# Sparse linear layer: the first weight piece in four row transfers on two queues, and the sixth token tile's load moved to ScalarE's queue

## The chip, the cores and the metric

One core of a Trainium2 chip. The metric is the device time of one execution in microseconds (us), lower is better; the median of several runs is compared. All starts below are us from the start of the profiled span. "Landed" is when a transfer's semaphore was complete, "issued" when the issuing engine began the DMA instruction.

## The reference

```
B, S, D = x.shape                      # x (16, 512, 1024), w (1024, 1024), b (1024), bf16
wg = w.reshape(D // 4, 4, D)           # groups of 4 neighbouring input rows
mag = jnp.abs(wg)
thr = second largest of mag in each group, for each output column
wp = (wg * (mag >= thr)).reshape(D, D) # keep 2 of 4
return jnp.einsum("bsd,df->bsf", x, wp) + b
```

So the weights have to be pruned on the chip before they can be used, and then 8192 tokens are multiplied by a 1024 x 1024 matrix.

## The kernel before, in words

The tokens are 64 tiles of 128. The output columns are two halves `h` of 512, the input rows two halves `g` of 512. A group's four rows lie side by side in the free dimension of the weight tiles `w_gh[(g, h)]` (128 partitions x 4 rows `m` x 512 columns), so that pruning is elementwise work on VectorE.

The front works on weight pieces: `pieces` 0 and 1 are columns 0 to 256 and 256 to 512 of `g` = 0, pieces 2 and 3 the next two quarters, pieces 4 and 5 the two halves of `g` = 1. For a piece, `abs_piece` takes the magnitude (an AND with 0x7FFF on VectorE, for piece 0 in two instructions, rows 0 and 1 and then rows 2 and 3; piece 3 on ScalarE), `prep_piece` computes the threshold (L131 to L138), the mask (L145) and the pruned weights (L148), for piece 0 again by two rows at a time. `load_w` (L71) loads columns of weights; it takes a range of rows `m0:m1`.

While pieces are pruned, TensorE transposes the first eight token tiles itself: `load_x` (L79) loads the first 512 columns of one or two token tiles, `transpose_half` (`T.t` in the list, four matmuls at L175) transposes tile `t` into a PSUM bank, `copy_half` (`C.t`, L180) copies it out on ScalarE, and `mm_part` (`N` and `M`, L196) multiplies it with a pruned piece. The tiles are counted from 0, so the sixth tile is tile 5.

The order of everything in the front is written out by hand in the string `FRONT`: each engine does its part of the list in that order. It begins with ten warm-up matmuls of 512 columns and two of 128 (`W`, `w`, L105), which need no data, and then

```
T.0 T.1 C.0 T.2 T.3 C.1 w T.4 T.5 C.2 N.0.0.0 N.0.0.1
N.0.1.0 N.0.1.1 N.0.2.0 N.0.2.1 N.0.0.2 N.0.0.3 ...
```

`N.0.t.m` is the product of tile `t` with row `m` of piece 0. The list then goes on with `C.4 C.5 M.0.3 N.0.4.0.1 T.6 T.7`, pieces 1 to 5, six further tiles whose tokens come by a transposing DMA (`xfill`, `load_fill`, L252), and copies of the pruned weights into their natural order `wp_nat` by DMA (`unpack`, `U`, L165). Partial sums are staged in SBUF (`to_stage`, `add_stage`, `add_bias`).

From 56 us on (L364) the remaining tiles run in batches of eight with transposing DMAs `xTb` two batches ahead (`issue_batch`, L264), 16 matmuls of 512 columns for each tile, and VectorE adding the bias out of PSUM (L241). Results of two tiles share a buffer `o_pair` (five of them); `half_done` writes a pair with one DMA of 512 KB from ScalarE's queue (L221), or, for the pairs in `singly`, with one of 256 KB after each tile (L214, L217).

Loads are issued by SyncE (SP) unless another engine is given; SyncE issues nearly all of them, in program order. Before the change ScalarE issues rows 2 and 3 of piece 0 and the tokens of tiles 2 and 3, then loads its function table, does a copy of 16 columns (`act_first`, L100), and turns to `C.0`. `K` keeps each engine's instructions in program order.

Of the kernel before, what the change touches and what calls it, by code (L numbers as in the profile page):

```python
# [10 lines left out]
def kernel(  # L11
# [7 lines left out]
    nc = tc.nc  # L19
# [49 lines left out]
    def load_w(g, c0, c1, eng=nc.sync, m0=0, m1=4):  # L69
        dst = w_gh[(g, c0 // FH)][:, m0:m1, c0 % FH:c0 % FH + c1 - c0]  # L70
        K(eng.dma_start(dst, wv[:, g, m0:m1, c0:c1]))  # L71
# [4 lines left out]
    def load_x(ta, tb, eng=nc.sync):  # L76
        xt = const.tile([P, tb - ta, KH], bf16, name=f"xh_{ta}")
        src = xf[ta * P:tb * P, 0:KH].rearrange("(t p) c -> p t c", p=P)
        K(eng.dma_start(xt[:], src))  # L79
        for t in range(ta, tb):  # L80
            xh[t] = xt[:, t - ta, :]

    load_w(0, 0, 256, nc.sync, 0, 2)
    load_w(0, 0, 256, nc.scalar, 2, 4)
    load_x(0, 2)
    load_x(2, 4, nc.scalar)
    load_x(4, 5)
    load_x(5, 6)
    load_w(0, 256, 512)
    load_x(6, 8)  # L90
    load_w(0, 512, 1024)
    bias_sb = const.tile([P, Dout], bf16, name="bias_sb")

    xg1 = const.tile([P, 4, T * P], bf16, name="xg1")
# [3 lines left out]
    K(nc.vector.memset(zeros[:], 0.0))  # L98
    act_first = const.tile([P, 16], bf16, name="act_first")
    K(nc.scalar.copy(act_first[:], zeros[:]))  # L100
    ident = const.tile([P, P], bf16, name="ident")
    make_identity(nc, ident[:])

# [100 lines left out]
            o_left[t // 2] = 2 if t == NT - 2 else 4  # L204
        return o_pair[t // 2][:, t % 2, :]

    singly = range(10, 17)

    def half_done(t):
        p = t // 2  # L210
# [188 lines left out]
```

## Time and profile before

| | |
|---|---|
| time, median of 3 runs | 233.31 us (233.16 to 233.41) |
| the profiled execution: its time / its span | 233.16 us / 231.4 us |
| TensorE busy | 227.9 us (98%) |
| VectorE, ScalarE, GpSimd busy | 120.4, 18.0, 0.7 us |
| DMA | 38.19 MB, mean 165 GB/s |
| granted TensorE clock | 0.999 |
| first matmul / first transpose (`T.0`) / first product (`N.0.0.0`) | 0.77 / 4.78 / 6.57 us |

The transfers of the first microseconds:

| transfer | queue | issued | landed |
|---|---|---|---|
| piece 0, rows 0 and 1 (128 KB) | SyncE | 0.73 | 3.53 |
| piece 0, rows 2 and 3 (128 KB) | ScalarE | 0.74 | 3.76 |
| tokens of tiles 0, 1 (256 KB) | SyncE | 1.25 | 4.74 |
| tokens of tiles 2, 3 (256 KB) | ScalarE | 1.26 | 5.24 |
| tokens of tile 4 (128 KB) | SyncE | 1.75 | 5.69 |
| tokens of tile 5 (128 KB) | SyncE | 2.25 | 6.07 |
| piece 1 (256 KB) | SyncE | 2.73 | 6.91 |
| tokens of tiles 6, 7 (256 KB) | SyncE | 3.44 | 8.67 |
| pieces 2 and 3 (512 KB) | SyncE | 4.10 | 11.02 |
| piece 4 (512 KB) | SyncE | 4.71 | 12.38 |
| `xfill`, first half (transposing) | SyncE | 5.38 | 16.77 |

In the profile PE is TensorE, PEld its weight loads, DVE VectorE, ACT ScalarE, POOL GpSimd, SP SyncE; a "q" behind the name means that the engine's issue side is meant. `q1` is SyncE's DMA queue and `q10` ScalarE's. A line of the timeline gives start, length, engine, source line, operation, output and input, and a count where like instructions are put together. Matmuls overlap: one of 256 columns is listed with 0.27 us, but the next begins 0.109 us later.

### The profile page before, as it was taken

Reading aid. Unit: us, or ns where it says so; the run is one execution under the profiler, and the core shown is the slowest. Engines: PE = TensorE matmul, PEld = TensorE weight load, DVE = VectorE, ACT = ScalarE, POOL = GpSimd, SP = SyncE. Lnnn points to the kernel's source line nnn. Section 1 sums busy time; section 2 is a strip of 40 time slices with the busy share of each in tenths; the row PEclk is TensorE's granted clock in tenths of the full one; section 3 lists DMA queues with packets and bytes.
Section 4 is the critical chain, followed back from the end, with each engine's and each line's share of the span. In section 5 each row is a group of like instructions: output and inputs, shape, how many; then the busy total and the mean of one; then the engine's idle time right before and its main releaser. Section 6 shows DMA issues by size and latency. Waiting matters only on the chain.

```text
span 231.4 us, 2786 instructions
## 1 busy us (share of the span) xinstructions
PE 227.9 (98%) x1156; PEld 110.8 (48%) x1156; DVE 120.4 (52%) x208; ACT 18.0 (8%) x33; POOL 0.7 (0%) x6
## 2 busy tenths in 40 slices
PE   8999999999999999999999999999999999999995
PEld 4887444444444444444444444444444444444443
DVE  3899887867987424424424424423423433433434
ACT  3777500000000000000000000000000000000000
POOL 1000000000000000000000000000000000000000
PEclk9999999999999999999999999999999999999999
DMA  6989998999957222991259622696129961122222
GB/s 208 264 179 233 218 192 177 267 258 270 320 189 272 91 95 70 235 284 58 81 129 251 164 93 92 137 241 192 68 91 200 224 211 40 53 91 91 91 93 91
DMA packets 77100, 38.19 MB, mean 165 GB/s; under 512 B 63136, under 2 KB 68896, under 8 KB 77088
## 3 DMA queue, kind: packets, MB, share of 16 engines
q1 hardware_dynamic: 67712, 20.91, 44.5%
q10 hardware_dynamic: 9376, 17.11, 20.4%
q8 instruction: 9, 0.15, 0.3%
q14 instruction: 3, 0.02, 0.0%
HBM read 3.41 MB, written 16.78 MB: 87 GB/s over the span
## 4 chain that ended last, share of the span: by engine, by line
PE 98%; DVE 0%; issue 0%
PE bank L364 73%; PE bank L196 17%; PE bank L256 6%; PE bank L105 2%; PE bank L175 1%; DVE o_last L347 0%
## 5 line engine op out<-in xcount | busy, mean ns | idle before, releaser
L364 PE MATMUL bank<-wp_nat,xTb 128*128 128x512 bf16 x752 | 162.5, 379 | 0.0
L241 DVE TENSOR_TENSOR o_pair<-bank,bias_sb 128x512 bf16<-128x512 f32 x104 | 67.3, 686 | 99.5 <-PE bank L364 96.3
L364 PEld LDWEIGHTS <-xTb 128*128 128x128 bf16 x752 | 73.6, 98 | 88.7
L232 DVE TENSOR_TENSOR stage<-bank,stage 128x512 f32<-128x512 f32 x22 | 14.4, 687 | 3.4 <-PE bank L196 3.3
L196 PE MATMUL bank<-w,xT 128*128 128x256 bf16 x128 | 14.5, 273 | 0.0
L196 PE MATMUL bank<-wp_nat,xg 128*128 128x512 bf16 x64 | 14.1, 379 | 0.0
L236 DVE TENSOR_TENSOR o_pair<-stage,bias_sb 128x512 bf16<-128x512 f32 x22 | 14.0, 683 | 0.0
L196 PEld LDWEIGHTS <-xT 128*128 128x128 bf16 x128 | 12.2, 98 | 1.8 <-ACT xT L180 0.2
L228 ACT COPY stage<-bank 128x512 f32<-128x512 f32 x22 | 11.4, 611 | 3.7 <-PE bank L196 3.7
L196 PE MATMUL bank<-wp_nat,xfill 128*128 128x512 bf16 x48 | 10.7, 379 | 0.0
L256 PE MATMUL bank<-wp_nat,xfill 128*128 128x512 bf16 x48 | 10.5, 379 | 0.0
L196 PEld LDWEIGHTS <-xg 128*128 128x128 bf16 x64 | 6.3, 98 | 7.5
L256 PEld LDWEIGHTS <-xfill 128*128 128x128 bf16 x48 | 4.7, 97 | 5.7
L196 PEld LDWEIGHTS <-xfill 128*128 128x128 bf16 x48 | 4.7, 98 | 5.4
L364 PE MATMUL bank<-wp_nat,xTs 128*128 128x512 bf16 x32 | 7.1, 379 | 0.0
L145 DVE TENSOR_TENSOR mask<-mag,thr 128x512 bf16<-128x512 bf16 (+2 forms) x9 | 5.5, 630 | 0.2
L148 DVE TENSOR_TENSOR w<-w,mask 128x512 bf16<-128x512 bf16 (+2 forms) x9 | 5.5, 630 | 0.2
L105 PE MATMUL bank<-const-bfloat16-1.0 128*128 128x512 bf16 (+1 forms) x12 | 4.4, 542 | 0.8 <-PEq L383 0.8
L364 PEld LDWEIGHTS <-xTs 128*128 128x128 bf16 x32 | 3.1, 98 | 3.8
L120 DVE TENSOR_SCALAR mag<-w 128x512 uint16<-128x512 uint16 (+2 forms) x6 | 2.7, 468 | 3.1 <-DMA w<-in_w_dram 3.1
L180 ACT COPY xT<-bank 128x512 bf16<-128x512 bf16 x8 | 4.1, 607 | 2.8 <-PE bank L175 2.8
L256 PE MATMUL bank<-wp_nat,xTb 128*128 128x64 bf16 (+3 forms) x40 | 3.7, 251 | 0.0
(20 smaller groups left out, 26.4 us busy)
## 6 DMA issues: line engine op xcount, KB each, us to landing
out_dram<-o_pair ACTq DMA_DIRECT2D x24, 512.0 KB, 2.8
out_dram<-o_pair ACTq DMA_DIRECT2D x15, 256.0 KB, 2.1
wp_nat<-w SPq DMA_DIRECT2D x16, 128.0 KB, 2.9
w<-in_w_dram SPq DMA_DIRECT2D x3, 512.0 KB, 6.9
xh<-in_x_dram SPq DMA_DIRECT2D x2, 256.0 KB, 4.4
xh<-in_x_dram ACTq DMA_DIRECT2D x1, 256.0 KB, 4.0
xh<-in_x_dram SPq DMA_DIRECT2D x2, 128.0 KB, 3.9
w<-in_w_dram SPq DMA_DIRECT2D x1, 256.0 KB, 4.2
```

The source lines that it names most:

```text
L105: K(nc.tensor.matmul(bank[7][:, :n], lhsT=ones[:, :P], rhs=ones[:, :n], start=True, stop=True))
L120: K(nc.vector.tensor_single_scalar(mag[:, ms].bitcast(u16), w_of(i)[:, ms].bitcast(u16), 0x7FFF, op=Alu.bitwise_and))
L145: K(nc.vector.tensor_tensor(mask[:, ms], mag[:, ms], tb, op=Alu.is_ge))
L148: K(nc.vector.tensor_tensor(w_of(i)[:, ms], w_of(i)[:, ms], mask[:, ms], op=Alu.mult))
L180: K(nc.scalar.copy(xt[:], src))
L196: K(nc.tensor.matmul(dst, lhsT=lhs, rhs=rhs, start=c0 == 0 and m == 0, stop=c1 == FH and m == 3))
L228: K(nc.scalar.copy(stage[(h, t)][:], bank[own[(h, t)]][:]))
L232: K(nc.vector.tensor_tensor(st, bank[own[(2 + h, t)]][:], st, op=Alu.add))
L236: K(nc.vector.tensor_tensor(get_o(t)[:, f], stage.pop((h, t))[:], bias_sb[:, f], op=Alu.add))
L241: K(nc.vector.tensor_tensor(get_o(t)[:, f], bank[bk][:], bias_sb[:, f], op=Alu.add))
L256: K(nc.tensor.matmul(bank[bk][:, :c1 - c0], lhsT=xN[t][:, kt, :], rhs=wp_nat[h][:, kt, c0:c1], start=kt == 0, stop=kt == KT - 1))
L364: K(nc.tensor.matmul(bank[bks[h]][:], lhsT=xN[t][:, kt, :], rhs=wp_nat[h][:, kt, :], start=kt == 0, stop=kt == KT - 1))
```

## The change

Piece 0 is loaded by four transfers of one row each, rows 0 and 2 from SyncE and rows 1 and 3 from ScalarE. The tokens of tile 5 are issued by ScalarE, after its first copy in program order, and no longer by SyncE between tile 4 and piece 1. In program order the loads of tiles 6 and 7 and of pieces 2 and 3 now stand behind that; on SyncE's own queue their order is the same. Pairs 10 and 11 of the output are written as pairs.

```diff
-    load_w(0, 0, 256, nc.sync, 0, 2)
-    load_w(0, 0, 256, nc.scalar, 2, 4)
+    for m in range(4):
+        load_w(0, 0, 256, nc.scalar if m % 2 else nc.sync, m, m + 1)
     load_x(0, 2)
     load_x(2, 4, nc.scalar)
     load_x(4, 5)
-    load_x(5, 6)
     load_w(0, 256, 512)
-    load_x(6, 8)
-    load_w(0, 512, 1024)
     bias_sb = const.tile([P, Dout], bf16, name="bias_sb")
...
     K(nc.scalar.copy(act_first[:], zeros[:]))
+    load_x(5, 6, nc.scalar)
+    load_x(6, 8)
+    load_w(0, 512, 1024)
     ident = const.tile([P, P], bf16, name="ident")
...
-    singly = range(10, 17)
+    singly = range(12, 17)
```

## The prediction

> **What bounds the kernel now.** I read the page's busy shares first, then the chain of waits, then the timeline of the first 10 us by engine, and last the transfers one by one. T0, T1, ... are the token tiles; "T5's transposes" are the four L175 matmuls of the sixth tile.
>
> ```profile
> PE 227.9 (98%) x1156; PEld 110.8 (48%) x1156; DVE 120.4 (52%) x208; ACT 18.0 (8%) x33; POOL 0.7 (0%) x6
> PE 98%; DVE 0%; issue 0%
> ...
> PEld L196 <- ACT xT L180: 0.2, 1, 0.2
> PEld L175 <- DMA xh<-in_x_dram: 0.2, 1, 0.2
> ```
>
> TensorE starts at 0.77 and never stops; only two short waits after the warm-up stand on its side. So the time is TensorE's stream plus the holes in it, and the whole effect of the change must be a hole opened or closed. Holes to close: the starts of the single matmuls, where they are further apart than their own 109 ns or 56 ns, give 0.05 us at 6.57 (first product, pruned rows ready at 6.52), 0.06 at 7.07 (C.2's copy), 0.01 at 7.19, 0.07 at 7.37 (second half of the pruned rows), 0.07 at 8.71 to 8.80 (T6's load), 0.03 at 10.3 to 10.4: 0.29 us, of which 0.24 lie behind the first product. That is all that any earlier load can win.
>
> ```profile
> 4.78 1.40 PE L175 MATMUL bank<-ident,xh 128*128 128x128 bf16 x16
> 6.02 0.22 PE L105 MATMUL bank<-const-bfloat16-1.0 128*128 128x128 bf16 x1
> 6.07 0.61 PE L175 MATMUL bank<-ident,xh 128*128 128x128 bf16 x8
> 6.57 2.27 PE L196 MATMUL bank<-w,xT 128*128 128x256 bf16 x18
> 8.71 0.64 PE L175 MATMUL bank<-ident,xh 128*128 128x128 bf16 x8
> ```
>
> Read this against the landings: T0 begins at 4.78 with its load landed at 4.74; T5 begins at 6.30 with its load landed at 6.07 (cover 0.23); T6 begins at 8.71 with its load at 8.67. TensorE's order is fixed: T5's transposes stand in front of all products, so if T5's tokens are late, everything is late.
>
> ```profile
> xh<-in_x_dram SPq DMA_DIRECT2D x1, 128.0 KB, 3.8
> ...
> w<-in_w_dram SPq DMA_DIRECT2D x1, 256.0 KB, 4.2
> ...
> 1.79 1.28 ACT L100 ACT_TABLE_LOAD   x1 [1.79 <-issue]
> 3.09 0.20 ACT L100 COPY act_first<-zeros 128x16 bf16<-128x16 bf16 x1
> ...
> q10 hardware_dynamic: 85, 0.09, 96.7%
> q1 hardware_dynamic: 18, 0.01, 12.7%
> ```
>
> The first two are T5's load (issued 2.25, landed 6.07) and the second weight piece (issued 2.73, landed 6.91). The last two are the queues between 4.00 and 4.25: ScalarE's queue (q10), with T2/T3's load issued at 1.26, takes 85 packets, while SyncE's (q1) nearly stands still, though T4's load was issued on it at 1.75. Landings come in the order of issue over both queues: 3.53, 3.76, 4.74, 5.24, 5.69, 6.07, 6.91, 8.67. So I treat the two queues as one line, in which place goes by time of issue. The data run 3 to 4 us behind the issue: a transfer issued a little later loses nothing unless it loses its place.
>
> **The change, part by part.**
>
> *Four row transfers for two.* Same 256 KB. SyncE's list keeps its count up to the first weight pieces (two rows, T0/T1, T4, instead of one half, T0/T1, T4, T5; issues of 0.43 to 0.46 us), so the second piece would be issued at about 2.7 as now; T0/T1 and T4 are issued 0.45 later, T2/T3 on ScalarE 0.5 later. Bounds: if bytes alone count, nothing moves, since the line is already full from 2.5 (331 to 385 GB/s in the half-microsecond windows from 2.5 to 4.5). If each start has a price of its own, the first packets of the first four transfers (1.84, 2.32, 2.85, 3.28, about 0.48 apart) would put T0's load up to 0.97 later. I take near the first bound, 0 to 0.2, because in the full stretch the packets, not the starts, set the pace. A gain for the pruning: the first AND needs rows 0 and 1, but the chain goes on only after the second, which needs row 3; VectorE's step at 4.11 came 0.35 after the landing at 3.76. I put row 3 between 3.5 and 4.1, so pruning from -0.25 to +0.35; below, that lies in the shade of T5. T0 too: it may slip to 6.0 before it passes a T5 that waits until 7.25, since 21 slots of 56 ns fit between.
>
> *T5's tokens on ScalarE's queue, behind its first copy.* Taken off SyncE: one issue of 0.43, made up for by the second row. On ScalarE: two rows and T2/T3 take until about 2.25, the table load follows (1.28) to 3.55 and the 16-column copy to 3.8. If the issue waits for these, it falls at 3.6 to 3.85. There is a second brake: the trace has eight semaphores for loads, and its ninth transfer (the 512 KB weight piece, issued at 4.10) waits for the first one's landing. T5's load is now the eighth or ninth. As the ninth it can't be issued before the first row has landed, which I put at 3.0 to 3.5. Either brake places it behind the second weight piece (issued at 2.7), and perhaps behind or beside T6/T7's (3.4). A line in which T5's 128 KB and the piece's 256 KB change places lets T5 land where that piece landed: 6.91. Beside T6/T7's load it is up to 7.56, when 13 of that load's 16 parts had landed. I take the middle, 7.2.
>
> Working: T5 begins at 7.25 instead of 6.30; its four transposes take 0.22; the first product begins at 7.47 instead of 6.57: +0.90. The 0.24 of holes behind it close, as copies, pruning and T6's load do not wait for TensorE there. Net +0.66. Ends: landing at 6.91 gives 7.18, +0.61 - 0.24 = +0.37; at 7.56 it gives 7.83, +1.26 - 0.24 = +1.02.
>
> What is late next: nothing. T6/T7's and the 512 KB loads follow the same number of bytes as before (8.67, 11.02), and their users start 0.66 later. Behind those, VectorE and ScalarE start the third and fourth pieces on the landing at 11.02, with 0.05 of cover at TensorE's 14.23 and none at 15.11; and the unpacked rows of 26.07 meet a matmul at 26.18. All that cover grows by 0.66. If T5 is not late, it is thin, and half of it is a hole of 0.1 to 0.3.
>
> *SyncE's list behind it.* If the second piece is the ninth transfer, it waits for a row until 3.0 to 3.5, up to 0.8 later; its first packet came only at 4.93, so that is hidden. The token transpose then begins at up to 6.2 instead of 5.38. It lasts 7.73 there and 3.35 for the same size at 25.8, so it is held by the full line until 13.11 and not by its start. Zero, and 0.3 if that cover fails.
>
> *Output of pairs 10 and 11 in one transfer each.* Removes two issues of 0.35 on a ScalarE that is idle there. The joint transfer leaves with the second tile: 512 KB land in 2.8 alone (256 KB: 2.0) and in 8.2 beside a token transpose (the one at 146.85), so pair 11, issued at 91.6, lands near 99.8. Its buffer is used again five pairs on, at tile 32, about 118. A transpose beside joint writes took 14.1 instead of 13.2, so batch 32 lands at 104.6, for 118. Zero, with over 10 us of cover.
>
> **Sum.** The profiled execution is 231.4 of span plus 1.76 around it, 233.16, the fastest of the three; +0.66 on the median of 233.31 gives 233.97.
>
> **Rivals.**
> *On time.* ScalarE issues T5's load ahead of its copy, straight behind T2/T3's at about 2.35, and it is the eighth transfer; it keeps its place before the second piece and lands at 5.7 to 6.25. For it: VectorE's queue took the wait for the third addition at 29.84 while the second had not begun (30.09), so an engine's issue side does run past a step that waits only for the engine. Against: that is one step, and no table load is seen there. Result -0.1 to +0.2, 233.2 to 233.5, on the other side of the line: decided by whether T5's load is issued before 2.7. The Trainium skill, Perfetto Trace Analysis, DVE / Act Engine Instruction, speaks for this: the sequencer goes on once it has pushed an instruction into the queue. By that alone the sum is about zero. The trace agrees for VectorE (29.84 before 30.09); no row shows it for a table load.
> A second way to the same result: the two queues share each DMA engine by turns, so that T5's load, alone on its queue, passes the pieces. For it: T0's and T2's loads overlapped from 3.28 to 4.0. Against: the 85 to 18 packets above. The Trainium skill, DMA: Bandwidth & Descriptors, Queues, rings and completion order, states these turns, packet by packet; the windows at 4.00 speak against turns for loads that are issued one after the other.
> *Rows early.* Row 3 lands by 3.5, T5 is on time, and holes close: at best -0.29, 233.02.
> *Starts cost.* T5 on time, but each start costs 0.48: T0 at 5.75, then 25 slots of 56 ns, first product at 7.15, +0.58 - 0.24 = +0.34, 233.65.
> *Behind the stragglers.* T6/T7's load had three parts at 8.26 to 8.67, with packets of 1.3 to 1.6 us. If T5's load is behind it or catches these, T5 begins at 8.72: first product 8.94, +2.37 - 0.24 = +2.13, 235.4.
>
> **How the numbers follow.** Late T5: 0.56, of which 0.10 land so early that it stays within 0.2% (0.47 us, about what a measurement of this kernel can tell from no change). On time, by either way: 0.24. Rows early: 0.06, nearly all of it put as faster, since another execution may hold more than these 0.29. Starts cost: 0.06, half of it slower. Stragglers: 0.08. Slower 0.46 + 0.03 + 0.08 = 0.57; same 0.10 + 0.24 + 0.03 + 0.01 = 0.38; faster 0.05. The range takes late T5 (233.68 to 234.33), on time and the first half of the stragglers' stretch: 233.1 to 234.9.
>
> **What would show it.** T5's load issued by ScalarE after 3.0; its landing after that of the second weight piece; a wait "DMA xh" of 0.6 to 1.3 ahead of L175 at 6.3 to 7.3, and none at 7.07, 7.37, 8.71; after 10 us every start later by the same amount. Wrong, if T5's load is issued before 2.7, if T0 waits at 4.78 by more than 0.2, or if a hole opens at 14.2, 15.1 or 26.2.

## The result, and the profile after

| | median of 8 runs | from .. to | profiled execution: time / span |
|---|---|---|---|
| before | 233.18 us | 232.82 .. 233.41 | 233.16 / 231.4 us |
| after | 234.50 us | 233.77 .. 235.47 | 234.01 / 232.2 us |

The changed kernel is slower: the ratio is 1.0064, with an interval of 1.0041 to 1.0088, and the medians differ by 1.32 us. The runs of before lie within 0.6 us, those of after spread over 1.7 us. Three executions of after were profiled, and they show different parts of that spread: the one of the table, at 0.85 us above before's 233.16, and the two taken later (`e8_after_again`, +0.69, and `e12_after_third`, +1.79).

The page of after, its busy shares and the chain of waits by engine:

```profile
PE 226.7 (98%) x1137; PEld 110.7 (48%) x1156; DVE 120.4 (52%) x208; ACT 18.0 (8%) x33; POOL 0.7 (0%) x6
PE 95%; DMA 2%; ACTq 1%; issue 1%; DVE 0%; ACT 0%
```

TensorE is still busy for 98% of the span (19 matmul records are missing from this trace), but 2% of the chain is now a DMA, and its pieces name it: the load of the sixth tile's tokens.

```profile
2.90 4.42 DMA xh<-in_x_dram
```

TensorE's timeline of after (start, length, what; in brackets the idle time before and what ended it):

```profile
5.77 1.08 PE L175 MATMUL bank<-ident,xh 128*128 128x128 bf16 x16 [0.80 <-DMA xh<-in_x_dram]
...
6.75 0.39 PE L175 MATMUL bank<-ident,xh 128*128 128x128 bf16 x4
7.37 0.41 PE L175 MATMUL bank<-ident,xh 128*128 128x128 bf16 x4 [0.24 <-DMA xh<-in_x_dram]
7.62 2.13 PE L196 MATMUL bank<-w,xT 128*128 128x256 bf16 x18
```

Two loads are late, not one. T0 waits first (its load landed at 5.72 instead of 4.74; 14 of its 16 parts by 4.99), and T5 waits again behind T4 (landed at 7.32 instead of 6.07). ScalarE's timeline shows how T5's load was issued:

```profile
2.15 1.28 ACT L97 ACT_TABLE_LOAD   x1 [2.15 <-issue]
2.90 0.35 ACTq L79 DMA_DIRECT2D xh<-in_x_dram  x1
3.44 0.20 ACT L97 COPY act_first<-zeros 128x16 bf16<-128x16 bf16 x1
```

It went out at 2.90, in the middle of the table load and ahead of the copy, directly after row 0 had landed at 2.88.

The starts of TensorE's steps in the three profiled executions of after, as differences from before, show where the time comes from:

| | T0 | T2 | T4 | T5 | first product | T6 | time |
|---|---|---|---|---|---|---|---|
| before, start | 4.78 | 5.57 | 6.07 | 6.30 | 6.57 | 8.71 | 233.16 |
| forecast | 0 | 0 | 0 | +0.95 | +0.90 | +0.66 | +0.66 |
| after | +0.99 | +0.67 | +0.67 | +1.07 | +1.05 | +0.87 | +0.85 |
| after again | +0.99 | +0.68 | +0.68 | +0.68 | +0.62 | +0.67 | +0.69 |
| after, third | +0.77 | +1.29 | +1.32 | +1.99 | +1.97 | +1.80 | +1.79 |

Each row ends in its own time: what is lost by T6 at about 9 us is the whole loss. T0's 0.99 shrinks to 0.67 by T2, because 16 transposes that begin later run at TensorE's full rate from the start (1.08 us instead of 1.40; that rate came at 5.49 in before and at 4.82 here). T5 adds 0.40 to that in the first execution, nothing in the second, and 0.67 in the third.

The transfers whose landings (in us) matter in what follows:

| | before | after | after again | after, third |
|---|---|---|---|---|
| piece 0, last row or half | 3.76 | 3.62 | 3.57 | 3.55 |
| T0, T1 | 4.74 | 5.72 | 5.73 | 5.51 |
| T2, T3 | 5.24 | 5.91 | 6.09 | 6.82 |
| T5: issued / landed | 2.25 / 6.07 | 2.90 / 7.32 | 2.89 / 6.86 | 3.03 / 8.24 |
| piece 1 | 6.91 | 8.04 | 7.73 | 8.52 |

### The profile page after: what moved, and what is told of

It reads as the page before. It is cut to its first block, busy times and chain, and to the rows that moved or that the text cites. A ratio compares the mean times of both kernels' runs of the same rounds, so it can differ in the third digit from the quotient of the medians.

```text
span 232.2 us, 2766 instructions
## 1 busy us (share of the span) xinstructions
PE 226.7 (98%) x1137; PEld 110.7 (48%) x1156; DVE 120.4 (52%) x208; ACT 18.0 (8%) x33; POOL 0.7 (0%) x6
## 4 chain that ended last, share of the span: by engine, by line
PE 95%; DMA 2%; ACTq 1%; issue 1%; DVE 0%; ACT 0%
PE bank L364 73%; PE bank L196 16%; PE bank L256 6%; DMA xh<-in_x_dram 2%; DVE o_last L347 0%; ACTq L71 0%; PE bank L175 0%; ACT L97 0%; ACTq L79 0%
```

## The experiments

Differences of starts and times below are against the profiled execution of before. Each profile is one execution, and ratios are of several, with a 95% interval. Line numbers differ by a few from kernel to kernel; L174 to L178 are the transposes, L195 to L199 the products.

**1. The rows alone** (`e1_rows`): before, with only the four row transfers.

```diff
-    load_w(0, 0, 256, nc.sync, 0, 2)
-    load_w(0, 0, 256, nc.scalar, 2, 4)
+    for m in range(4):
+        load_w(0, 0, 256, nc.scalar if m % 2 else nc.sync, m, m + 1)
```

> Only the four row transfers are taken over; the sixth tile's load (T5) stays on SyncE between tile 4 and the second piece, pairs 10 and 11 are written as before. If T5's late load carries the whole loss, this is within 0.2 us of before (233.2). If the two extra starts hold back the tokens behind them (tiles 0 and 1 landed at 5.72 instead of 4.74 in the profile after), T0 begins 0.6 to 1.0 late and the time is 0.3 to 0.7 us above before.

Measured: ratio 1.0059 (1.0041 to 1.0077), as much as the whole change. TensorE's timeline of it:

```profile
5.44 1.12 PE L175 MATMUL bank<-ident,xh 128*128 128x128 bf16 x16 [0.45 <-DMA xh<-in_x_dram]
...
6.45 0.61 PE L175 MATMUL bank<-ident,xh 128*128 128x128 bf16 x8
6.89 2.35 PE L196 MATMUL bank<-w,xT 128*128 128x256 bf16 x18
9.23 0.64 PE L175 MATMUL bank<-ident,xh 128*128 128x128 bf16 x8
...
11.69 0.49 PE L196 MATMUL bank<-w,xT 128*128 128x256 bf16 x3 [0.27 <-DVE w L148]
```

T4 and T5 follow T0 to T3 without a wait of their own (T5's load, still on SyncE, landed at 6.42). T0 is 0.66 late, the first product 0.32, T6 0.52 (right behind its own load, which landed at 9.18 instead of 8.67); then a hole opens at 11.69 behind the second piece, which was issued at 3.10 instead of 2.73 and landed at 8.53 (15 of its 16 parts by 7.19). That makes 0.94 of this execution's 1.09. So the loss needs no moved T5. But it is not put together as in after. With T5 still on SyncE, SyncE's list is one transfer longer: the second piece and the tokens of T6 and T7 were issued 0.37 and 0.38 later than before (3.10 and 3.82), in after 0.10 and 0.09 earlier (2.63 and 3.35). Of the 0.94, 0.32 stand before the first product, behind T0's tokens, and 0.62 behind those two loads. So the equal ratios do not show that T0's load weighs the same in both kernels.

**2. The tokens alone** (`e2_t5`): before, with only T5's load moved, as in the change (the two loads behind it keep their order on SyncE).

```diff
     load_x(4, 5)
-    load_x(5, 6)
     load_w(0, 256, 512)
-    load_x(6, 8)
-    load_w(0, 512, 1024)
...
     K(nc.scalar.copy(act_first[:], zeros[:]))
+    load_x(5, 6, nc.scalar)
+    load_x(6, 8)
+    load_w(0, 512, 1024)
```

> Only T5's load is moved to ScalarE behind its first copy; the first piece stays in two halves, pairs 10 and 11 are written as before. T5's load is now the seventh or eighth transfer, so no semaphore of an earlier one holds it. If that semaphore (waited for until 2.90 in the profile after) made it late, it is issued before 2.3 and lands near 6: time within 0.2 us of before. If ScalarE's queue itself makes it late, it lands at 7 or later and the time is 0.6 to 1.2 us above before.

Measured: ratio 1.0003 (0.9994 to 1.0012), no difference. ScalarE's timeline of it:

```profile
1.79 1.28 ACT L97 ACT_TABLE_LOAD   x1 [1.79 <-issue]
1.85 0.42 ACTq L79 DMA_DIRECT2D xh<-in_x_dram  x1
```

The issue at 1.85 waits neither for the table load nor for the copy, which began at 3.09. T5 landed at 6.42, and T4, now moving beside it, at 6.19 instead of 5.69; TensorE waited 0.27 for T4. T4 and T5 begin about 0.2 late, the first product 0.14, and T6 is 0.03 early. The on-time rival describes this kernel, and T5's move by itself costs nothing.

**3. The pairs alone** (`e3_pairs`): `singly = range(12, 17)` in before.

> Only pairs 10 and 11 are written as pairs. All theories of the front expect no change (within 0.15 us of before). If the joint writes collide with the token transposes, a wait of TensorE shows between 85 and 120 and the time rises by 0.2 or more.

Measured: ratio 1.0004 (0.9994 to 1.0013), nothing. Its profile shows how far a first product can move with no change in the front: TensorE came to its full rate at 6.41 instead of 5.49, the transposes took longer, and the first product began 0.38 later, of which 0.18 were left at 14 us.

**4. T5 taken out of the way** (`e4_t5_later`): after, with `T.5` moved in the list behind the first twelve products.

```diff
-        ... T.4 T.5 C.2 N.0.0.0 N.0.0.1
-        ... N.0.2.2 N.0.2.3 A.1 C.3 P.1
+        ... T.4 C.2 N.0.0.0 N.0.0.1
+        ... N.0.2.2 N.0.2.3 T.5 A.1 C.3 P.1
```

> The changed kernel, but T5's transposes stand behind the twelve first products in TensorE's order, so that a load landing at 7.3 has cover until about 8.5. If T5's late landing sets the loss, it falls from 1.3 us to 0.3 or less. If the late tokens of tiles 0 and 1 set it (T0 at 5.77), the first product comes at about 7.15 and 0.3 to 0.6 us stay; if those loads scatter from run to run, the scatter of 1.7 us between runs stays too.

Measured: ratio 1.0037 (1.0025 to 1.0049). T5's load landed at 7.97 for a step that began at 8.57. T0 was still 0.83 late, and T6 0.73. The larger part of the loss stays without any wait for T5; the interval overlaps that of after, so the 0.42 us between the medians (234.08 and 234.50) are a hint of T5's share, not a measurement.

**5. T5's load ahead of the brake** (`e5_t5_seventh`): after, with T5's load straight behind that of T2 and T3 on ScalarE, as the seventh transfer.

```diff
     load_x(2, 4, nc.scalar)
+    load_x(5, 6, nc.scalar)
     load_x(4, 5)
...
-    load_x(5, 6, nc.scalar)
```

> The changed kernel with T5's load straight behind that of tiles 2 and 3 in ScalarE's list, so that it is the seventh or eighth transfer and waits for no semaphore. If the wait for the semaphore until 2.90 is what makes T5 late, it is issued at about 2.15, lands before 6.7 and has no wait of its own; T0 still begins 0.5 to 1.0 late because of the four rows. If the loss of the changed kernel is T5's, the time falls to within 0.3 us of before; if it is carried by the late tokens of tiles 0 and 1 and what the rows delay besides, 0.7 to 1.3 us stay.

Measured: ratio 1.0066 (1.0043 to 1.0089), no better than after. It was issued at 2.14, so the wait for a semaphore was gone. TensorE's timeline of it:

```profile
6.95 1.08 PE L175 MATMUL bank<-ident,xh 128*128 128x128 bf16 x16 [1.96 <-DMA xh<-in_x_dram]
```

T4 and T5 follow (7.92) without a wait of their own; everything stands behind T0, whose load had 15 of its 16 parts by 5.44 and the last at 6.90. This execution took 235.01, so one late part can make a long execution. The loads behind T0's had a late last part too: T2/T3 at 7.08, T4 at 7.58 and T5 at 7.75 (15 parts by 6.66), so T5's early issue did not bring it in before 6.7 as expected.

**6. Two starts, almost no bytes** (`e6_two_tiny`): before, with a transfer of 16 rows of 32 bytes on each queue, ahead of the tokens. Nothing reads them.

```diff
     load_w(0, 0, 256, nc.scalar, 2, 4)
+    tiny = const.tile([P, 2, 16], bf16, name="tiny")
+    K(nc.sync.dma_start(tiny[:16, 0, :], xf[0:16, 0:16]))
+    K(nc.scalar.dma_start(tiny[:16, 1, :], xf[0:16, 0:16]))
     load_x(0, 2)
```

> The kernel before with two more transfers of 16 rows of 32 bytes, one on each queue, between the halves of the first piece and the tokens; nobody reads them. The bytes and rows of the first piece are as before, the number of transfers ahead of the tokens as in the changed kernel. If the number of starts (or the later issue, by 0.4) is the price, the tokens of tiles 0 and 1 land 0.5 to 1.0 late and the time rises by 0.6 to 1.3 us, as with the rows. If the form of the row transfers is (one row of 512 bytes for each partition), T0 begins at 4.78 to 5.0 and the time stays within 0.3 us of before.

Measured: ratio 1.0093 (1.0074 to 1.0111), more than the whole change, with the halves left as they were and 1 KB added. The windows show what the DMA engines did; first before, then after, then after once more (`e8_after_again`), then this kernel, from 3.0 on in steps of half a microsecond. The last column is what the DMA engines moved in GB/s, the one before it their busy share.

```profile
3.00:3.50 0.50, 0.50 (x3) 0.16 (x2) 0.00 (x0) 0.28 (x2) 0.00 (x0) 1.00 1.08 367
3.50:4.00 0.50, 0.50 (x2) 0.15 (x1) 0.45 (x2) 0.00 (x0) 0.00 (x0) 1.00 1.09 385
```

```profile
3.00:3.50 0.50, 0.50 (x3) 0.17 (x2) 0.29 (x1) 0.49 (x2) 0.00 (x0) 1.00 0.88 202
3.50:4.00 0.50, 0.50 (x2) 0.15 (x1) 0.32 (x2) 0.14 (x1) 0.00 (x0) 1.00 0.94 274
```

```profile
3.00:3.50 0.50, 0.50 (x3) 0.16 (x2) 0.29 (x1) 0.49 (x2) 0.00 (x0) 1.00 0.98 59
3.50:4.00 0.50, 0.50 (x2) 0.15 (x1) 0.38 (x2) 0.14 (x1) 0.00 (x0) 1.00 0.42 133
```

```profile
3.00:3.50 0.50, 0.50 (x3) 0.16 (x2) 0.20 (x1) 0.50 (x1) 0.00 (x0) 1.00 0.80 37
3.50:4.00 0.50, 0.50 (x2) 0.15 (x1) 0.47 (x3) 0.25 (x2) 0.00 (x0) 1.00 0.28 33
```

Before moves 367 and 385 GB/s there. With the rows it is 202 and 274 in one execution and 59 and 133 in another, and with the two tiny transfers 37 and 33: for a microsecond almost nothing moves, though the loads of T0 to T3 had been issued at 1.75 and 1.78. T0's load landed at 6.46, and T0 began 1.72 late:

```profile
6.51 1.90 PE L178 MATMUL bank<-ident,xh 128*128 128x128 bf16 x16 [1.52 <-DMA xh<-in_x_dram]
```

So neither the bytes of the rows nor their form is needed: two more transfers ahead of the tokens are enough. Three things limit this.

- An added transfer also puts the issue of T0's load later, by 0.50 here (1.75 instead of 1.25) and by 0.40 in after (1.65). No run delays the issue alone, so up to that much of the 1.72 may be the later issue.
- The load does not begin late. The tokens' packets have 1 KB and the weights' 512 bytes, so the trace shows its first packet: at 3.15 here and at 2.89 to 3.07 in the three profiles of after, against 2.85 before. In this execution and in the second profile of after, seven of its packets then last 0.7 to 1.1 us each, against 0.05 before, and so the engines count as busy (0.80 and 0.98) while they move little. In the third profile of after the packets are short and the engines partly idle (174 GB/s at a busy share of 0.59). One may read the rates as a price of each start that the bytes in front can hide, 128 KB wholly and a row of 64 KB in part, but the executions of one kernel lie too far apart (202, 59 and 174) to show that.
- Not all of this kernel's loss is that wait. In this execution (236.13) T6 began 2.86 late, 1.14 more than T0, because TensorE came to its full rate only at 10.07: the transposes of T0 to T5 ran 0.107 us apart instead of 0.056. The fastest execution of this kernel, 234.84, lies 1.6 above before.

**7. Three starts on one queue** (`e7_three_starts`): before, with rows 2 and 3 as two transfers, both on ScalarE.

```diff
     load_w(0, 0, 256, nc.sync, 0, 2)
-    load_w(0, 0, 256, nc.scalar, 2, 4)
+    load_w(0, 0, 256, nc.scalar, 2, 3)
+    load_w(0, 0, 256, nc.scalar, 3, 4)
```

> Three transfers for the first piece: rows 0 and 1 together from SyncE as before, rows 2 and 3 singly from ScalarE. SyncE issues the tokens of tiles 0 and 1 at 1.25 as before; ScalarE those of tiles 2 and 3 at 1.66. If the place in the own queue and its time of issue count, tiles 0 and 1 land at 4.7 and only tiles 2 and 3 come 0.2 to 0.4 later (cover 0.33): time within 0.3 us of before. If the starts of both queues add up, tiles 0 and 1 land 0.2 to 0.5 late and the time is 0.3 to 0.7 us above before.

Measured: ratio 1.0034 (1.0023 to 1.0046). TensorE's timeline of it:

```profile
4.78 1.06 PE L176 MATMUL bank<-ident,xh 128*128 128x128 bf16 x8
6.46 0.64 PE L176 MATMUL bank<-ident,xh 128*128 128x128 bf16 x8 [0.62 <-DMA xh<-in_x_dram]
```

T0's load, second on SyncE, landed at 4.67 as ever. T2's, third on ScalarE, landed at 6.41 instead of 5.24, and only the steps behind it are late (first product 0.86, T6 0.69). The loss is on the queue with the third start, though larger than I had expected.

**8. After once more** (`e8_after_again`): the changed kernel, profiled a second time.

> The changed kernel once more, for a second profile: its runs lay between 233.8 and 235.5. If the same wait decides in each execution, T5's load lands last before the first product again (7.0 to 8.7) with T0 at 5.4 to 6.0. If the scatter comes from single late parts of a load, another load may be the one that is waited for, and the first product moves by up to 1 us.

Measured: 233.85, one run. TensorE's timeline of it:

```profile
5.77 1.08 PE L175 MATMUL bank<-ident,xh 128*128 128x128 bf16 x16 [0.79 <-DMA xh<-in_x_dram]
...
6.75 0.61 PE L175 MATMUL bank<-ident,xh 128*128 128x128 bf16 x8
```

T0 begins as in the first profile, and T4 and T5 run through without a gap: with the same late issue (2.89) T5's load landed at 6.86, in time. Here T0's load alone decides.

**9. T5 late without more starts** (`e9_t5_behind_piece`): before, with T5's load and the second piece exchanged on SyncE.

```diff
     load_x(4, 5)
-    load_x(5, 6)
     load_w(0, 256, 512)
+    load_x(5, 6)
     load_x(6, 8)
```

> The kernel before, with T5's load and that of the second weight piece changing places in SyncE's list; nothing else. This is the step on which the forecast rests, without the rows. If a load takes the place in line of the one it is exchanged with, T5 lands at 6.8 to 7.0, T5 begins at 6.9 to 7.05, the first product at 7.1 to 7.3 and the time rises by 0.3 to 0.5 us. If loads overtake each other (parts on 16 engines), T5 lands below 6.6 and the time stays within 0.2 us of before.

Measured: ratio 1.0022 (1.0013 to 1.0031). A line of TensorE's timeline, and one of its weight loads later on:

```profile
6.77 0.41 PE L175 MATMUL bank<-ident,xh 128*128 128x128 bf16 x4 [0.21 <-DMA xh<-in_x_dram]
...
33.77 2.27 PEld L196 LDWEIGHTS <-xfill 128*128 128x128 bf16 x12 [0.45 <-DMA xfill<-in_x_dram]
```

The load was issued at 2.97, behind the piece, landed at 6.73, and the first product began 0.45 late (7.02), of which 0.20 was given back by 14 us. So a T5 that loses its place does cost about what its landing says. But the agreement of the time (233.66, +0.47) with my figure is partly chance: in the profiled execution 0.25 comes from T5 and 0.23 from holes at 26 and 33 us. Both stand behind a transposing load whose issue took 6.66 instead of 5.80: the first of the pruned rows that SyncE unpacks after it landed at 26.61 instead of 26.07, and `xfill`'s second transfer was issued at 26.42 instead of 25.82.

**10. Tokens second, rows behind them** (`e10_tokens_second`): four rows again, but rows 2 and 3 behind the loads of T0 to T3.

```diff
-    load_w(0, 0, 256, nc.sync, 0, 2)
-    load_w(0, 0, 256, nc.scalar, 2, 4)
+    load_w(0, 0, 256, nc.sync, 0, 1)
+    load_w(0, 0, 256, nc.scalar, 1, 2)
     load_x(0, 2)
     load_x(2, 4, nc.scalar)
+    load_w(0, 0, 256, nc.sync, 2, 3)
+    load_w(0, 0, 256, nc.scalar, 3, 4)
```

> Four row transfers, but the tokens stand second on each queue and rows 2 and 3 third. If the third start of a queue is late whatever it carries, tiles 0 and 1 land at 4.6 to 4.8 again and T0 begins at 4.78, rows 2 and 3 land at 4.7 to 5.5 instead of 3.6, the first product comes at 7.5 to 8.3 and the time rises by 0.8 to 1.6 us. If it is the tokens' transfers that suffer from rows ahead of them, tiles 0 and 1 land after 5.0 here too.

Measured: ratio 1.0074 (1.0061 to 1.0088). T0 began at 4.78, as in before. The first product in TensorE's timeline:

```profile
8.32 2.27 PE L198 MATMUL bank<-w,xT 128*128 128x256 bf16 x18 [1.64 <-DVE w L150]
```

The tokens are on time behind one row each (landed at 4.67 and 5.08), and the bill goes to what stands third: rows 2 and 3 landed at 5.30 and 5.50, the pruning was late, and the first product waited 1.64 for it. So one row ahead of the tokens on each queue does not hurt them, and what stands third is late. As rows 2 and 3 stand behind 256 KB each here, their own lateness holds bytes as well as a start.

**11. One start for piece 0** (`e11_one_start`): all of piece 0 in one transfer of 256 KB on SyncE, the tokens of T0 to T3 first on ScalarE.

```diff
-    load_w(0, 0, 256, nc.sync, 0, 2)
-    load_w(0, 0, 256, nc.scalar, 2, 4)
-    load_x(0, 2)
+    load_w(0, 0, 256)
+    load_x(0, 2, nc.scalar)
     load_x(2, 4, nc.scalar)
```

> The other direction: the first piece in one transfer of 256 KB from SyncE, the tokens of tiles 0 and 1 and of 2 and 3 first and second on ScalarE's queue. One start fewer ahead of the tokens. If starts are the price, the tokens of tiles 0 and 1 land before 4.5 and no wait for tokens stands before the first product; the piece lands at 3.5 to 4.0, pruning is 0.1 earlier to 0.2 later: time 233.0 to 233.4, at best 0.2 us better than before.

Measured: ratio 1.0069 (1.0056 to 1.0082); the expectation failed. T0's load landed at 3.62, over a microsecond early, and it did not help: the piece landed at 5.08, and the first product began at 8.10, behind the pruning:

```profile
8.10 2.26 PE L195 MATMUL bank<-w,xT 128*128 128x256 bf16 x18 [0.85 <-DVE w L147]
```

The first packets tell why. Both transfers were issued at 0.73, on different queues; T0's began to move at 1.83, the piece's only at 2.65. I had assumed that first transfers on two queues start side by side. They started one after the other. The distance is not a fixed price of a start: it was 0.48 in before (1.84 and 2.32) and 0.18 in after (1.77 and 1.95), where the first two transfers have 128 KB and 64 KB each instead of 256.

**12. After a third time** (`e12_after_third`), for the long executions.

> A third profiled execution of the changed kernel, for the spread of its times (233.77 to 235.47). Theory (starts ahead of the tokens): the load of tiles 0 and 1 lands at 5.4 to 5.8, T0 begins 0.6 to 1.0 late, 233.8 to 234.6; if it falls among the executions near 235.4, single parts of one load land over 1 us behind its other parts, of tiles 0 and 1 (T0 near 6.9, first product near 8.3) or of tile 5 (first product near 8.3 with T0 at 5.8). Rival (late T5 makes the long executions): T0 at 5.8 or earlier and a wait of over 1 us ahead of T5.

Measured: 234.95, one run. TensorE's timeline of it:

```profile
5.56 0.89 PE L175 MATMUL bank<-ident,xh 128*128 128x128 bf16 x8 [0.57 <-DMA xh<-in_x_dram]
6.86 0.64 PE L175 MATMUL bank<-ident,xh 128*128 128x128 bf16 x8 [0.42 <-DMA xh<-in_x_dram]
...
8.29 0.42 PE L175 MATMUL bank<-ident,xh 128*128 128x128 bf16 x4 [0.51 <-DMA xh<-in_x_dram]
```

Three token loads are late here, one behind the other: T0 by the usual amount, T2 because the last parts of its load were scattered (13 of 16 by 5.54, the rest at 6.03, 6.50 and 6.82), and T5 with its load at 8.24 (half of it by 7.04). Of the 1.99 at T5, 1.32 had been lost before it and 0.67 is its own. The theory's long case, scattered parts, and the rival's, a late T5, both have a share in this one, though the wait ahead of T5 was 0.51 and not over 1 us.

## Why the prediction was right, and where its steps were not

The forecast was slower, 233.97 in a range of 233.1 to 234.9; the measured 234.50 lies inside, about twice as far from before as I had put it (1.32 against 0.66). The direction came out through a term that I had sized near zero, while the term that was to carry the loss, T5's late load, gave 0.40, 0 and 0.67 in the three profiles. So it is in part luck that the time lies in the range.

*Four row transfers.* This is the step that failed: "I take near the first bound, 0 to 0.2, because in the full stretch the packets, not the starts, set the pace." T0's load landed 0.77 to 0.99 later in the three profiles of after and 0.65 later with the rows alone. The other bound, 0.97 from the spacing of the first packets, had about the right size, but not the mechanism: it would have put the first packet of T0's load 0.97 later, and that came only 0.04 to 0.22 later (2.89 to 3.07 instead of 2.85). What came late is the rest: less moved from 3.0 on (202, 59 and 174 GB/s in the three profiles, where before has 367), and the parts landed further apart (4.52 to 5.72 in after, 4.36 to 4.74 in before). Experiment 1 shows that the rows alone lose as much as the whole change, experiments 4 and 5 that with T5 out of the way much or all of the loss stays, and experiment 6 that two more transfers of almost no bytes are enough. The Trainium skill, DMA: Bandwidth & Descriptors, Issuing engines are not separate DMA queues, says that issuing from several engines only saves the time of the issue, usually small beside the transfer. The trace agrees that the queues are no independent ways in (first packets at 1.83 and 2.65 in experiment 11), but here two more transfers, one on each queue, cost more than the time of their issue: T0's load was issued 0.40 to 0.50 later and landed 0.65 to 1.7 later.

*Starts cost, as a rival.* The mechanism was named, with a chance of 0.06 and +0.34; the price was too small. Nor was it 0.48 for each start: the first packets of the first two rows were 0.18 apart. Its sum let T0's transposes run at 56 ns from 5.75 on, which they did, and took off 0.24 of holes closed, which they did not: where T0's load decides ("after again"), first product to T6 took 2.18 us against 2.14 before, because the copies behind the transposes moved too (TensorE's weight loads waited 0.3 for one of them). Without that 0.24, its +0.58 stands beside +0.62 measured in that profile.

*T5's tokens.* Right in part. The semaphore brake did hold the issue, as ninth transfer, until the first row had landed (2.90 behind 2.88). The other brake, the copy, does not exist, and my condition for the on-time case, issue before 2.7, was met in experiment 2 and not in after. The Trainium skill, Perfetto Trace Analysis, DVE / Act Engine Instruction, has the sequencer go on once it has pushed its instruction into the queue; the trace agrees, for a table load too (1.85 inside 1.79 to 3.07). The landing of 7.32 was inside my 6.91 to 7.56, the first product's +1.05 near my +0.90, and the holes gave back 0.21 of the 0.24. But the agreement in that one profile hides that T4 before it was already 0.67 late: T5's own share was 0.40 there, 0 and 0.67 in the others. And it needs the rows: T5 moved alone costs nothing, and T5 issued early in after (experiment 5) wins nothing.

*One line over both queues.* I concluded from the order of landings that place goes by time of issue. First packets do come one after the other across the queues (experiment 11), but not strictly by time of issue: in after, ScalarE's first row was issued at 0.73 and moved at 1.95, SyncE's at 0.74 and 1.77. For the packets behind them it does not hold either: in after, 12 of 16 parts of T5's load landed by 6.12, ahead of half of piece 1 (7.12), though issued 0.27 later.

*T0 in the shade of T5.* I let T0 slip to 6.0 free of charge because T5 would wait longer. It held in the first profile and the third and not in the second, where T5 was on time and T0's lateness showed in full.

*SyncE's list, the pairs, what is late next.* The pairs cost nothing (experiment 3). SyncE's list cost nothing in after: no hole at 14.2, 15.1 or 26.2. A later second piece is not always hidden, though: in experiment 1, where it was issued at 3.10, one late part of it (8.53) opened the hole at 11.69. And the thin cover behind 20 us is real: experiment 9 lost 0.23 there.

*Of the signs to watch,* T5's issue after 3.0 was met in one of the three (2.90, 2.89 and 3.03), its landing was behind that of piece 1 in none, the wait ahead of it was 0.24, none and 0.51 instead of 0.6 to 1.3, and the sign that I had named as the end of my account, T0 waiting at 4.78 by more than 0.2, is there in all three (0.80, 0.79, 0.57).

What stays open is why more transfers ahead hold the engines back, how much of it is the later issue alone, and why the parts of a load scatter by up to 1.5 us in some executions. That this scatter sets the spread of after (233.77 to 235.47) fits the long executions of experiments 5 and 12, but is not shown. No run here changes that scatter by itself. T5's share of the median is not settled either: experiment 4 puts it at 0.4 us, with overlapping intervals, and experiment 5 at nothing.

## What to carry to other kernels

Before splitting a first load, count how many transfers must start ahead of the data that the first real work waits for: a split that keeps the bytes can still make that data late, by 0.65 to 1 us here for one more transfer on each of two queues. A full DMA rate in the profile of before is no proof that more transfers are free. When a change has several parts, run each part alone: here the part that looked dangerous had a visible wait in the profile and cost nothing by itself.

## What was not expected of the hardware

- Two transfers of half a kilobyte, one on each queue, left the DMA engines at 33 to 37 GB/s for a microsecond, with 640 KB already issued behind them by 2.25; for half of it the engines counted as 0.80 busy, with single packets of up to 1.1 us.
- First transfers that were issued at the same time on two queues began to move 0.82 us apart (1.83 and 2.65) with 256 KB in each, 0.48 with 128 KB and 0.18 with 64 KB.
- ScalarE's queue issues a DMA while the engine loads its function table (1.85 within 1.79 to 3.07, 2.90 within 2.15 to 3.43).
- Single parts of a load can land far behind the others: 6.90 after 15 parts by 5.44 (experiment 5), 8.53 after 15 by 7.19 (experiment 1).
- TensorE's step to its full rate came at 5.49 in before, at 4.69 in experiment 4, at 6.41 in experiment 3 and at 10.07 in experiment 6, by the clock's record in the trace; where T0 to T3 followed each other without a wait, their 16 transposes took from 1.08 (after) over 1.40 (before) to 1.94 us (experiment 11).
